# ScalarE scales the states' part of an mLSTM output, and the first unit's work is reordered

## The chip, the cores and the metric

The kernel runs on one core of a Trainium2 chip. A core has five engines that matter here, each with its own instruction queue: TensorE (PE, matmuls and transposes; PEld is its loading of weights), VectorE (DVE), ScalarE (ACT), GpSimd (POOL), and SyncE (SP), which here issues most of the DMA transfers. [...] The metric is device microseconds of one execution; several executions are made, and the median is given.

## The reference

Two blocks run one after the other. The first is an mLSTM cell over 4 batches, 8 heads, 768 tokens and a head dimension of 40; the second is a feed-forward network in which two up-projections are multiplied.

```python
for t in range(S):
    m_new = np.maximum(f_gate[:, :, t] + m, i_gate[:, :, t])
    f_stab = np.exp(f_gate[:, :, t] + m - m_new)
    i_stab = np.exp(i_gate[:, :, t] - m_new)
    m = m_new
    C = f_stab * C + i_stab * einsum('bhd,bhe->bhde', vt, kt)
    n = f_stab * n + i_stab * kt
    h_tilde = einsum('bhde,bhe->bhd', C, qt)
    denom = np.maximum(np.abs(einsum('bhd,bhd->bh', n, qt)), 1.0)
    y[:, :, t] = sigmoid(o_gate[:, :, t]) * h_tilde / denom
x = y.transpose(0, 2, 1, 3).reshape(3072, 320)
a = x @ w1                      # 320 -> 1024
b = x @ w2                      # 320 -> 1024
return ((a * b) @ w3) @ w_out   # 1024 -> 1024 -> 320
```

## The kernel before

**The cell.** Time is cut into units of 128 tokens of one batch with all 8 heads. There are 24 units; unit n is chunk n // 4 of batch n % 4. Within a unit the recurrence is written as matrix products over two halves of 64 tokens. For each head:

- The scores `ss` are k·q, multiplied by a masked weight `pw` (an exponential that ScalarE takes at L280 and GpSimd masks at L282). The product is made by VectorE at L355, straight from PSUM.
- `pc` is the unit's contribution to the state: `vw` (v times a gate weight, GpSimd, L304) times k.
- One step later, `ph` is the product of the weighted scores with v, and `pi` is the state times q. The unit's output is h = ph + pi·gT, where gT is a gate column, one value per token and head. An appended column of ones gives the denominator in the same products, so a head has 41 columns.

On VectorE the output `outputs(n)` is L377 (pi times gT, all heads in one instruction), four additions L382 (ph), three small ones on the denominator (L390 to L393), L398 (the output gate, whose tanh ScalarE takes at L263), and L400, which writes y. GpSimd then copies y's last columns (L430), and PE transposes y (`px`), which ScalarE copies to `xT` (L440).

**The feed-forward part.** The weights arrive as 64-bit words. ScalarE scales the raw words (L178), and four VectorE instructions make fp32 of them (L189 to L192). w3 and w_out are folded into one matrix w3o on the chip (`wp`, evicted by ScalarE at L257). The up-projections are the PSUM tiles `pa` and `pb`; ScalarE evicts `pa` to `a_sb` (L585) and VectorE multiplies it with `pb` into `ab` (L586).

**The steps.** A loop over s = 0 to 31 puts the two blocks beside each other. Step s issues the loads of unit s+2, transposes k and q of unit s (PE `pt`; ScalarE copies them to `kT` and `qT`, L299, for units below 10, and VectorE transposes them itself from unit 10 on), takes one fold of w3 and the up-projections (one or two pairs from step 4 on), and then calls `quarter_work(s)`. That finishes the up-projections (a_sb and ab), then issues PE's `ph` and `pi` of unit s-1, `ss` and `pc` of unit s, and the VectorE work on them. At the end of the step ScalarE takes the exps of unit s+1 and the tanh of unit s, and weights are converted and fetched.

The order of the instructions on ScalarE, VectorE, GpSimd and SyncE is the order in which the program writes them (`keep_order`), from the gate scans to step 31; PE is in order as well. PE's results other than the cell's lie in four PSUM banks, taken in rotation, so that in steps with two pairs of up-projections the first `pb` takes the bank of k's `pt` and waits until ScalarE has copied it to `kT`. The cell's own results lie in two tiles `cell` of two banks each: `ph` and `pi` in one, `ss` and `pc` in the other.

**Before the loop** VectorE scans the gates (L514 to L528), and `gate_cols` transposes the gate rows into columns `aT`, `wT` and `gT`. `spread(0)` puts the first unit's gate values into PSUM, and `weights(0)` takes the exps and masks them.

In `quarter_work` the order on VectorE before the change is: L377 and the four L382 of unit s-1, L355 of unit s, the state (L360 or L362), the denominator of unit s-1, the second state addition (L368), L398 and L400.

Of the kernel before, what the change touches and what calls it, by code (L numbers as in the profile page):

```python
# [10 lines left out]
AF = mybir.ActivationFunctionType  # L11
OP = mybir.AluOpType
# [4 lines left out]
def kernel(  # L17
# [26 lines left out]
    nc = tc.nc  # L44

    B, H, S, D = q.shape
    L = 64
# [53 lines left out]

    NB, NBQ = 4, 3
    N_DVE = 10
    q_all = const.tile([P, NBQ * H * DP], FP, name="q_all")
    qbuf = [q_all[:, i * H * DP:(i + 1) * H * DP].rearrange("p (h d) -> p h d", d=DP) for i in range(NBQ)]
    kbuf = [const.tile([P, H, DP], FP, name=f"kbuf{i}") for i in range(NB)]
# [4 lines left out]
    gT = const.tile([P, NT2, BH], FP, name="gT")  # L111
    wT = const.tile([P, NT2, BH], FP, name="wT")
# [38 lines left out]
    def weights_tile(n):  # L151
        if n not in u_t:
            u_t[n] = io.tile([P, H, L], FP, name="pw", tag="pw", bufs=5)
        return u_t[n]
# [71 lines left out]
    def scale_next():  # L226
        scaled.append(pend.pop(0))
        scale(scaled[-1][1])
# [36 lines left out]
    def spread(n):  # L265


        ub = mps([P, H, L], "ub")
        for h in range(H):
            r = n % B * H + h  # L270
            for x in range(2):
                mm(ub[halves[x], h, :], ident[0:RG, r:r + 1].to_broadcast([RG, L]), U[:, x * L:(x + 1) * L])
        return ub

    def weights(n):
        c, b = divmod(n, B)
        src = weights_tile(n) if c else spread(n)
        pw = weights_tile(n)
        for h in range(H):
            nc.scalar.activation(out=pw[:, h, :], in_=src[:, h, :], func=AF.Exp, bias=aT[:, c, b * H + h:b * H + h + 1])  # L280
        for r in halves:
            nc.gpsimd.affine_select(out=pw[r], in_=pw[r], compare_op=OP.is_ge, fill=0.0, base=0,  # L282
                                    pattern=[[0, H], [1, L]], channel_multiplier=-1)
# [17 lines left out]
    def weighted(n):  # L301
        c, b = divmod(n, B)
        vw_t[n] = sb.tile([P, H, D1], FP, name="vw", tag="vw")
        nc.gpsimd.tensor_tensor(out=vw_t[n], in0=vbuf[n % NB], op=OP.mult,  # L304
                                in1=wT[:, c, b * H:(b + 1) * H].unsqueeze(2).to_broadcast([P, H, D1]))
# [6 lines left out]
    def quarter_work(s, rest):  # L312


        rest()

        def part(j, c0, n):
            return cell[j][:, :, c0:c0 + NP * n].rearrange("p x (n d) -> p x n d", d=n)

        ss, pc, pi = part(0, 0, L), part(0, NP * L, D1), part(1, 0, D1)  # L320
        ph = [cell[1][:, x, NP * D1:2 * NP * D1].rearrange("p (h d) -> p h d", d=D1) for x in range(2)]
        n = s - 1
        if 0 <= n < NU:
            pw, vt, qT = u_t.pop(n), vbuf[n % NB], qT_t.pop(n)
            before = before_t.pop(n)

            for hd in range(H // 2):
                for x, e in quarters:
                    hq = hd if x == e else hd + H // 2
                    mm(ph[x][halves[e], hd, :], pw[halves[x], hq, :], vt[halves[x], hq, :])  # L330
            for p in range(NP):
                for hip, x in quarters:
                    mm(pi[halves[x], hip, p, :], qT[heads[hip], p, halves[x]], before[x][heads[hip], p, :])
        n, first_read = s, None
        if n < NU:
            c, b = divmod(n, B)
            kt, vw = kbuf[n % NB], vw_t.pop(n)
            ends = range(2 if c < NT2 - 1 else 1)
            first, second, after = state[b]
            before_t[n] = first, second  # L340
            state[b] = after, second, first
            kT, qT, pw = kT_t.pop(n), qT_t[n], u_t[n]
            for p in range(NP):
                for hip, x in quarters:
                    mm(ss[halves[x], hip, p, :], kT[heads[hip], p, halves[x]], qT[heads[hip], p, halves[x]])
            for p in range(NP):
                for x, e in quarters:
                    if x in ends:
                        mm(pc[halves[e], x, p, :], kt[halves[x], 2 * p + e, :], vw[halves[x], 2 * p + e, :])
        den = None  # L350
        if 0 <= s - 1 < NU:
            den = outputs(s - 1, pi, ph)
        if n < NU:
            pv = pw.rearrange("p (n two) t -> p two n t", two=2)
            first_read = nc.vector.tensor_tensor(out=pv, in0=ss, in1=pv, op=OP.mult)  # L355
        with tc.issue_after(first_read.ins) if first_read else nullcontext():
            if n < NU:

                if c:
                    nc.vector.tensor_tensor(out=second, in0=pc[:, 0], in1=second, op=OP.add)  # L360
                else:
                    nc.vector.tensor_copy(out=second, in_=pc[:, 0])  # L362
                if len(ends) > 1:
                    decayed(after, second, n, 1)
            if den:
                done = den()
            if n < NU and len(ends) > 1:
                nc.vector.tensor_tensor(out=after, in0=pc[:, 1], in1=after, op=OP.add)  # L368
            if den:
                done = done()  # L370
        return done if den else first_read

    def outputs(n, pi, ph):
        c, b = divmod(n, B)
        hs = slice(b * H, (b + 1) * H)
        h = sb.tile([P, H, D1], FP, name="h", tag="h")
        nc.vector.tensor_tensor(out=h.rearrange("p (n two) d -> p two n d", two=2), in0=pi,  # L377
                                in1=gT[:, c, hs].rearrange("p (n two) -> p two n", two=2).unsqueeze(3)
                                .to_broadcast([P, 2, NP, D1]), op=OP.mult)
        for x, e in quarters:  # L380
            part = h[halves[x], 0:H // 2] if x == e else h[halves[x], H // 2:H]
            nc.vector.tensor_tensor(out=part, in0=ph[x][halves[e]], in1=part, op=OP.add)  # L382

        den = sb.tile([P, H, 1], FP, name="den", tag="den")

        def first():
            V = nc.vector
            V.tensor_scalar(out=den.bitcast(U32), in0=h[:, :, D:D1].bitcast(U32), scalar1=0x7FFFFFFF, scalar2=None,  # L390
                            op0=OP.bitwise_and)
            V.tensor_scalar(out=den, in0=den, scalar1=1.0, scalar2=2.0, op0=OP.max, op1=OP.mult)
            V.reciprocal(out=den, in_=den)  # L393
            return then

        def then():
            e = o_t.pop(n)
            nc.vector.scalar_tensor_tensor(out=e, in0=e, scalar=1.0, in1=den.to_broadcast([P, H, D]), op0=OP.add, op1=OP.mult)  # L398
            y_t[n] = sb.tile([P, DM + REM], FP, name="y", tag="y")
            return nc.vector.tensor_tensor(out=y_t[n][:, 0:DM].rearrange("p (h d) -> p h d", d=D), in0=h[:, :, 0:D],  # L400
                                           in1=e, op=OP.mult)

        return first
# [39 lines left out]
    GR, GC = 3, NT // 3  # L443
    TC = GC * L
    RG = GR * BH
# [6 lines left out]
    w, g = f_sb, on  # L452
# [58 lines left out]
    V = nc.vector  # L511
# [19 lines left out]
    def gate_cols(src, dst, copy):  # L531
        pg = mps([P, GC // 2, GR, BH], "pg")
        for c in range(GC // 2):
            transpose(pg[:, c].rearrange("p g r -> p (g r)"), src[:, c * P:(c + 1) * P], RG)
        for c in range(GC // 2):
            copy(out=dst.rearrange("p (g c) r -> p c g r", g=GR)[:, c], in_=pg[:, c])

    turn(0)
    gate_cols(a, aT, nc.scalar.copy)
    nc.scalar.activation(out=dec, in_=U3[:, :, L - 1], func=AF.Exp)  # L540
    scale_next()
    V.tensor_tensor(out=w3d, in0=a3, in1=U3[:, :, L - 1:L].to_broadcast([RG, GC, L]), op=OP.add)
    scale_next()
    convert()
    nc.scalar.activation(out=w, in_=w, func=AF.Exp)

    for i, r in enumerate(third):
        nc.gpsimd.tensor_tensor(out=pick[r, :, i, :], in0=pair[r].to_broadcast([BH, B * NP, GC]), op=OP.mult,
                        in1=dec[r].unsqueeze(1).to_broadcast([BH, B * NP, GC]))
    weights(0)  # L550
    pd = mps([P, B * NP * NT], "pd")
    for x in range(2):
        mm(pd[halves[x]], odd[:, x].to_broadcast([RG, L]), pick.rearrange("p j g c -> p (j g c)"))
    gate_cols(w, wT, nc.scalar.copy)
    nc.scalar.copy(out=decay.rearrange("p j c -> p (j c)"), in_=pd)
    nc.scalar.activation(out=g, in_=U, func=AF.Exp)
    scale_next()
# [151 lines left out]
    for s in range(len(n_up)):  # L709
# [6 lines left out]
            weights(s + 1)  # L716
            out_gate(s)
        if s < NU:
            weighted(s)
            if s >= B:  # L720
                decayed(state[s % B][1], state[s % B][0], s, 0)
            if 0 < s < N_DVE:
                turn(s)
# [109 lines left out]
```

## Time and profile before

Three executions took 443.79, 445.97 and 446.03 us; the median is 445.97. The span of the profiled execution is 444.0 us.

| What | Value |
|---|---|
| Busy: PE, PEld | 420.7 us, 332.6 us |
| Busy: DVE, ACT, POOL | 342.8, 133.8, 81.7 us |
| Instructions: DVE, ACT, POOL | 704, 376, 154 |
| L377 (pi times gT) | 24 times, 0.490 us each |
| L382 (four additions, one unit) | 1.35 us |
| L355 (the product pw) | 0.69 us |
| L280 (exps), data in SBUF | 160 times, 0.335 us each; eight in 2.00 us |
| L280 (exps), data in PSUM | 32 times, 0.322 us each; eight in 1.71 us |
| Start of the cell's PE work in steps 7, 8, 9, 10 | 83.41, 96.73, 109.00, 126.04 us |

The profile is read in this way. Busy times are per engine and add up over the span; a share of 95% for PE says that the engine is hardly ever idle, not that it works at its peak. Neighbouring ScalarE instructions overlap, so eight exps of 0.335 us take 2.00 us and not 2.68; the distance from start to start (the pitch) is what a queue behind them feels. A view of waits lists, for an engine, what released it when it had been idle; a timeline gives each instruction's start and length, with the idle time before it in brackets.

### The profile page before, as it was taken

What the parts mean: (1) busy time and instruction counts of PE and PEld (TensorE: products, weight loads), DVE (VectorE), ACT (ScalarE), POOL (GpSimd) and SP (SyncE); (2) the same over time, 40 slices, a digit from 0 to 9 for tenths busy, and PEclk for the clock granted to TensorE, in tenths of its full rate; (3) what the DMA queues carried; (4) which work ended last, traced back from release to release, by engine and by line L of the source; (5) the groups of instructions that cost most, each with busy time, mean ns of one, the idle gap of its engine ahead of it and who ended that gap; (6) DMA issues with size and microseconds to landing.
All of it is one profiled execution on the core that took longest, in us unless ns stands there. A gap on an engine that the chain in (4) does not pass through costs nothing.

```text
span 444.0 us, 12907 instructions
## 1 busy us (share of the span) xinstructions
PE 420.7 (95%) x5271; PEld 332.6 (75%) x5271; DVE 342.8 (77%) x704; ACT 133.8 (30%) x376; POOL 81.7 (18%) x154
## 2 busy tenths in 40 slices
PE   4778998999999999999999999999999999999997
PEld 3666777788678788887877877878778777777774
DVE  6699999989998988898867859659699776444800
ACT  3655445534342244133302320213211111101110
POOL 3362433123220220222022203202010000000000
PEclk9998999999999999999999999999999999999999
DMA  8999979888988787688466477274111120000001
GB/s 204 186 184 214 191 127 165 159 193 185 194 196 191 162 169 169 157 158 154 98 113 144 94 143 144 68 132 110 50 35 35 40 45 17 15 16 15 1 30 44
DMA packets 136554, 52.71 MB, mean 119 GB/s; under 512 B 109936, under 2 KB 127536, under 8 KB 136496
## 3 DMA queue, kind: packets, MB, share of 16 engines
q1 hardware_dynamic: 132896, 47.87, 54.7%
q10 hardware_dynamic: 3600, 4.03, 2.7%
q8 instruction: 41, 0.67, 0.7%
q14 instruction: 17, 0.14, 0.1%
HBM read 46.07 MB, written 5.80 MB: 117 GB/s over the span
## 4 chain that ended last, share of the span: by engine, by line
PE 75%; DVE 8%; SPq 6%; DMA 4%; issue 2%; POOL 2%; ACT 1%; DVEq 0%; ACTq 0%; POOLq 0%
PE cell L92 22%; PE pa L92 17%; PE po L92 14%; PE pb L92 11%; PE wp L92 7%; PE p L92 5%; SPq L173 3%; DMA raw<-in_moe_w_dram 2%; DMA raw<-in_moe_w_out_dram 1%; DVE h L382 1%; DMA o_in<-in_o_gate_dram 1%; DVE pw L355 1%; DVE ex L189 1%; SPq L137 1%; DVE ma L191 1%
## 5 line engine op out<-in xcount | busy, mean ns | idle before, releaser
L92 PE MATMUL po<-w3o,ab 128*128 128x320 f32 x224 | 61.8, 433 | 0.0
L92 PE MATMUL pa<-xT,w 128*128 128x256 f32 x240 | 60.5, 383 | 0.9 <-ACT xT L440 0.8
L92 PEld LDWEIGHTS po<-w3o,ab 128*128 128x128 f32 x224 | 42.4, 190 | 17.3 <-issue 0.4
L309 POOL TENSOR_TENSOR state<-state,decay 128x164 f32<-128x164 f32 x40 | 19.7, 492 | 181.2 <-DVE den L390 178.8
L92 PEld LDWEIGHTS pa<-xT,w 128*128 128x128 f32 x240 | 44.5, 190 | 8.6 <-ACT xT L440 1.5
L92 PE MATMUL pb<-xT,w 128*128 128x256 f32 x192 | 45.6, 380 | 1.6 <-ACT kT L299 1.5
L282 POOL TENSOR_SCALAR_AFFINE_SELECT pw<-pw 64x512 f32<-64x512 f32 x48 | 35.1, 732 | 52.4 <-ACT pw L280 47.9
L92 PE MATMUL cell<-w3o,ab 128*128 128x320 f32 x160 | 44.0, 432 | 0.0
L92 PEld LDWEIGHTS pb<-xT,w 128*128 128x128 f32 x192 | 36.3, 190 | 7.2 <-ACT kT L299 2.4
L280 ACT ACTIVATE pw<-pw,aT 128x64 f32<-128x64 f32 x160 | 40.2, 336 | 2.9 <-ACT o_sb L688 2.9
L633 DVE SCALAR_TENSOR_TENSOR a_sb<-pa,wo 128x512 f32<-128x512 f32 x12 | 8.3, 691 | 42.2 <-PE pa L92 42.2
L92 PEld LDWEIGHTS cell<-w3o,ab 128*128 128x128 f32 x160 | 30.4, 190 | 12.0
L585 ACT ACTIVATE a_sb<-pa 128x512 f32<-128x512 f32 x24 | 14.3, 598 | 77.7 <-PE pb L92 77.7
L92 PE MATMUL wp<-wo,w3T 128*128 128x320 f32 x128 | 35.9, 433 | 1.0 <-DVE ab L586 1.0
L92 PE MATMUL pa<-xT,wr 64*64 64x256 f32 x384 | 36.8, 386 | 0.0
L92 PE MATMUL pb<-xT,wr 64*64 64x256 f32 x384 | 36.2, 379 | 0.0
L382 DVE TENSOR_TENSOR h<-cell,h 64x164 f32<-64x164 f32 x96 | 31.3, 326 | 1.8
L92 PEld LDWEIGHTS wp<-wo,w3T 128*128 128x128 f32 x128 | 23.7, 190 | 10.1 <-DVE ab L586 1.2
L92 PEld LDWEIGHTS pa<-xT,wr 64*64 64x64 f32 x384 | 19.0, 132 | 14.4 <-issue 8.3
L688 ACT COPY o_sb<-po 128x320 f32<-128x320 f32 x14 | 6.0, 425 | 67.4 <-PE po L92 67.4
L586 DVE TENSOR_TENSOR ab<-pb,a_sb 128x512 f32<-128x512 f32 x24 | 16.4, 688 | 8.6 <-ACT a_sb L585 8.4
L92 PE MATMUL cell<-vw,kbuf 64*64 64x41 f32 x704 | 16.4, 227 | 6.6 <-POOL vw L304 4.4
(123 smaller groups left out, 738.2 us busy)
## 6 DMA issues: line engine op xcount, KB each, us to landing
raw<-in_moe_w_dram SPq DMA_DIRECT2D x64, 128.0 KB, 3.2
pw<-U_d SPq DMA_DIRECT2D x40, 128.0 KB, 3.8
kbuf<-in_k_dram SPq DMA_DIRECT2D x24, 160.0 KB, 4.6
vbuf<-in_v_dram SPq DMA_DIRECT2D x24, 160.0 KB, 4.8
o_in<-in_o_gate_dram SPq DMA_DIRECT2D x24, 160.0 KB, 4.8
out_dram<-o_sb ACTq DMA_DIRECT2D x24, 160.0 KB, 1.8
raw<-in_moe_w_dram SPq DMA_DIRECT2D x7, 512.0 KB, 6.1
raw<-in_moe_w_out_dram SPq DMA_DIRECT2D x32, 80.0 KB, 3.3
```

The costliest lines, as they stand in the source:

```text
L92: in_order(nc.tensor.matmul(out, lhsT=lhsT, rhs=rhs, start=start, stop=stop))
L137: nc.sync.dma_start(out=dst[p0:p0 + 32, c0:c0 + NP * RAW].rearrange("r (p e) -> r p e", p=NP), in_=of.rearrange("p (r f) d -> r p (f d)", ...
L173: nc.sync.dma_start(out=dst, in_=src)
L189: V.tensor_scalar(out=t, in0=hi, scalar1=3, scalar2=None, op0=OP.logical_shift_left)
L280: nc.scalar.activation(out=pw[:, h, :], in_=src[:, h, :], func=AF.Exp, bias=aT[:, c, b * H + h:b * H + h + 1])
L282: nc.gpsimd.affine_select(out=pw[r], in_=pw[r], compare_op=OP.is_ge, fill=0.0, base=0, pattern=[[0, H], [1, L]], channel_multiplier=-1)
L309: nc.gpsimd.tensor_tensor(out=new, in0=old, op=OP.mult, in1=decay[:, b * NP:(b + 1) * NP, 2 * c + x:2 * c + x + 1] .to_broadcast([P, NP, D1]))
L382: nc.vector.tensor_tensor(out=part, in0=ph[x][halves[e]], in1=part, op=OP.add)
L585: nc.scalar.mul(out=a_sb, in_=pa, mul=UP ** -2)
L586: nc.vector.tensor_tensor(out=ab_t[gr][j][:, fs[0]:fs[-1] + 1, t0:t0 + a_sb.shape[-1]], in0=pb, in1=a_sb, op=OP.mult)
L633: nc.vector.scalar_tensor_tensor(out=out, in0=p, scalar=UP ** -2, in1=q, op0=OP.mult, op1=OP.add)
L688: nc.scalar.copy(out=o_sb, in_=po)
```

## The change

The change has two parts. For units 0 to 15 the product of the states' part with the gate column (L377) goes from VectorE to ScalarE: eight activations, one for each head, each with the head's gate column as its scale. VectorE's remaining work on the output is put off: the scores' product L355 and the state come first, then the four additions, the denominator, and the rest. In ScalarE's order the eight stand behind the step's `a_sb` evictions and ahead of the exps of the next unit, the tanh, the raw scales and the next step's copies `kT` and `qT`.

The second part is the first unit. The gate weight's exponent (`w3d`) and exp are taken ahead of the first raw scale, `spread(0)` and the transposes `wT` right behind it; GpSimd makes `vw` of unit 0 ahead of the masks of `weights(0)`, and PE makes `pd` (the decay columns) after that.

It is meant to relieve VectorE, which is busy 77% of the span, by using ScalarE, which is busy 30%, and to let the first scores' product begin earlier.

```diff
+    N_ACT = 16
...
-    def weights(n):
+    def weights(n, src=None):
         c, b = divmod(n, B)
-        src = weights_tile(n) if c else spread(n)
+        src = src or (weights_tile(n) if c else spread(n))
...
             if den:
                 done = den()
+                if s <= N_ACT:
+                    done = done()
             if n < NU and len(ends) > 1:
                 nc.vector.tensor_tensor(out=after, in0=pc[:, 1], in1=after, op=OP.add)
...
         h = sb.tile([P, H, D1], FP, name="h", tag="h")
+        if n < N_ACT:
+            for hd in range(H):
+                nc.scalar.activation(out=h[:, hd, :], in_=pi[:, hd % 2, hd // 2, :], func=AF.Copy,
+                                     scale=gT[:, c, b * H + hd:b * H + hd + 1])
+            return lambda: outputs_rest(n, h, ph)
         nc.vector.tensor_tensor(out=h.rearrange("p (n two) d -> p two n d", two=2), in0=pi,
...
+        return outputs_rest(n, h, ph)
+
+    def outputs_rest(n, h, ph):
         for x, e in quarters:
...
+    V.tensor_tensor(out=w3d, in0=a3, in1=U3[:, :, L - 1:L].to_broadcast([RG, GC, L]), op=OP.add)
+    nc.scalar.activation(out=w, in_=w, func=AF.Exp)
     scale_next()
-    V.tensor_tensor(out=w3d, in0=a3, in1=U3[:, :, L - 1:L].to_broadcast([RG, GC, L]), op=OP.add)
+    first_spread = spread(0)
+    gate_cols(w, wT, nc.scalar.copy)
     scale_next()
     convert()
-    nc.scalar.activation(out=w, in_=w, func=AF.Exp)
...
-    weights(0)
+    weighted(0)
+    weights(0, first_spread)
     pd = mps([P, B * NP * NT], "pd")
...
-    gate_cols(w, wT, nc.scalar.copy)
     nc.scalar.copy(out=decay.rearrange("p j c -> p (j c)"), in_=pd)
...
         if s < NU:
-            weighted(s)
+            if s:
+                weighted(s)
```

## The prediction

> **What bounds the kernel now.** I read the page first, then the waits of TensorE (PE) by stretches, then the timelines of ScalarE (ACT) and PE where a wait ends, then the windows. The page:
>
> ```profile
> PE 420.7 (95%) x5271; PEld 332.6 (75%) x5271; DVE 342.8 (77%) x704; ACT 133.8 (30%) x376; POOL 81.7 (18%) x154
> ```
>
> PE is busy for 420.7 of 444.0 us, so all that a change on other engines can win is some 20 us of gaps. The waits of PE between 16 and 124 us (line, releaser: us in total, times, longest):
>
> ```profile
> PE cell L92 <- POOL vw L304: 4.4, 3, 2.9
> PE cell L92 <- issue: 2.2, 3, 1.0
> PE px L95 <- POOL y L430: 1.9, 2, 1.1
> PE pb L92 <- ACT kT L299: 1.5, 1, 1.5
> PE wp L92 <- DVE ab L586: 1.0, 1, 1.0
> ```
>
> The same view from 124 to 444 us is empty: in that stretch PE waits for nothing, and nothing off PE can shorten it. So I ask one thing: does the change move the moment at which PE passes 120.6 us, after which it never waits? The windows (start:end, length; busy PE, PEld, DVE, ACT, POOL; PE clock, DMA share, GB/s):
>
> ```profile
> 30.00:40.00 10.00, 7.29 (x225) 6.33 (x218) 9.56 (x22) 5.98 (x16) 4.25 (x7) 0.83 1.06 174
> 40.00:60.00 20.00, 16.61 (x346) 13.65 (x345) 18.45 (x40) 9.26 (x26) 7.38 (x12) 1.00 1.15 192
> 100.00:124.00 24.00, 22.90 (x244) 18.20 (x243) 22.98 (x48) 9.42 (x23) 6.80 (x12) 1.00 0.95 191
> ```
>
> Up to 124 us the DMA share is about one, and DVE is busy 92 to 96% of the time. The queue of SyncE runs without a break from 9.7 to 124 us; for its transfers I looked for the last reader or writer of each buffer, and none was the reason that a transfer began (the closest was done 1.4 us earlier). So transfers, not engines, set the pace there. They pin PE at three places: A, the transposes of unit 4's k begin at 39.77, its k landing at 39.64; B, PE pb at 76.26, behind ACT, whose scaling of raw words waits for a transfer that lands at 75.14; C, the stretch before 120.61:
>
> ```profile
> 113.88 0.68 ACT L178 ACTIVATE raw<-raw 128x512 f32<-128x512 f32 x1 [1.23 <-DMA raw<-in_moe_w_dram]
> 117.78 0.69 ACT L178 ACTIVATE raw<-raw 128x512 f32<-128x512 f32 x1 [3.21 <-DMA raw<-in_moe_w_dram]
> 119.52 0.69 ACT L178 ACTIVATE raw<-raw 128x512 f32<-128x512 f32 x1 [1.05 <-DMA raw<-in_moe_w_dram]
> 120.10 0.47 ACT L440 COPY xT<-px 128x384 f32<-128x384 f32 x1
> ```
>
> Between B and C stands the place that decides, the ACT queue of step 8 and the PE groups behind it:
>
> ```profile
> 96.96 0.60 ACT L585 ACTIVATE a_sb<-pa 128x512 f32<-128x512 f32 x1 [0.27 <-PE pb L92]
> 97.45 2.00 ACT L280 ACTIVATE pw<-pw,aT 128x64 f32<-128x64 f32 x8
> 99.36 0.46 ACT L263 ACTIVATE o_in<-o_in 128x320 f32<-128x320 f32 x1
> 99.72 1.61 ACT L178 ACTIVATE raw<-raw 128x320 f32<-128x320 f32 x3
> 101.23 0.56 ACT L299 COPY kT<-pt 128x512 f32<-128x512 f32 x1
> ```
> ```profile
> 99.94 1.89 PE L92 MATMUL pa<-xT,w 128*128 128x256 f32 x8
> 101.84 1.99 PE L92 MATMUL pb<-xT,w 128*128 128x256 f32 x8
> ```
>
> ACT has no gap from the second a_sb to kT, and PE pb starts at 101.84, 0.05 after kT has freed its bank at 101.79. PE itself was ready at 101.66 (99.94 plus 8 starts of 0.2155). ACT has no slack here, though it is busy only 30% of the span.
>
> **What the Trainium skill says.** The Trainium skill, "ScalarE: Activation LUTs", section What ACT_TABLE_LOAD costs: an activation with one [128,1] pointer operand takes about 280 ns + 0.833 ns an element, and neighbours overlap by about 93. For the 64-element exps that is 333 alone and 240 from start to start; the trace has a median of 335 and a pitch of 0.239 us, so it agrees for data in SBUF. For 41 elements the page gives an estimate of 314 ns, a pitch of 0.221. "PSUM — Partial Sum Buffer", section Engine vs sequencer instructions: the queues of ScalarE, VectorE and GpSimd are strictly first in, first out, and matmuls start in program order; the timeline above agrees, kT's copy waiting behind work that has nothing to do with it. "TensorE: Matmul & The Clock Gate", Part 1: after an idle window of about 3.4 us PE runs at half rate; the clock of 0.83 in the window 30 to 40 fits.
>
> **The change, part by part.**
>
> (1) Sixteen times, 8 ACT activations of 41 elements from PSUM take the place of one DVE product. Their price is not in the trace. The first unit's exps read PSUM: 8 of 64 elements took 1.71 us, a pitch of 0.196. Raw scales of 512 and 320 elements give some 0.9 ns an element, so 23 fewer take off 0.02: pitch 0.175, eight cost **1.4 us**. Lower end 1.0 (pitch 0.13, as short copies have), upper end 1.8 to 1.9 (the page's 0.221, or 0.239 as from SBUF). I take 1.4, since source and operands match that row best. No further table load is expected: the copies of L299 already stand between exps, and the trace has one table load in all.
>
> (2) DVE loses L377, 0.49 us in each of 16 stages. The page's DVE is nearly full before 124 us, so this is time that DVE gets; but what DVE gives earlier ends at pins A, B and C.
>
> (3) Scores first: the product pw (0.69) no longer stands behind 0.49 + 1.34 us of h work, but waits for the last pc matmul, about 0.8 us after pi. y of the unit then comes about 1.35 us later relative to pw. Queued behind it are POOL's copy of y (L430) and PE's px, a step later, with a stage of 11 to 13 us between: hidden from unit 6 on.
>
> (4) First unit. The chain shows its price:
>
> ```profile
> 14.18 1.02 POOL pw L282
> 15.27 0.74 POOL vw L304
> 16.06 1.14 PE cell L92 x32
> 17.32 0.69 DVE pw L355
> ```
>
> With wT's transposes and vw ahead of the exps and selects, vw ends near 11.9 in place of 16.0, and pw's product starts near 15.4 in place of 17.32, bound by the second select: **1.9 us** earlier. Units 1 to 3 come earlier by as much, and unit 4 by nothing, since its k lands at 39.64 as before (pin A). PE idles longer before that, which costs up to one 3.4 us window at half clock.
>
> (5) What follows. After A, the waits for POOL y (0.8 and 1.1) shrink, against the ACT delay of 1.4 in each step; up to stage 6 this comes to between -0.35 and +0.5. At B the transfer decides: 0 to +0.2, as the eight stand ahead of the raw scale in the queue, long done when it lands.
> Step 7: pi ends near 84.5, the eight follow, kT moves from 88.12 to 89.9; PE pb stood at 89.68, so +0.27.
> Step 8: pi ends near 97.88, that is 0.43 after ACT was free at 97.45; 0.43 + 1.4 = 1.83 of delay, plus 0.27: kT ends near 103.9, and pb moves from 101.84 to 103.94, **+2.1**. Behind that wait PE has all of step 8's second half queued.
> Step 9: PE waited 0.97 for DVE ab (L586) before wp at 112.48. DVE is ahead by then, so this wait is eaten: +1.1. At C the transfer chain left PE 0.28 of slack (pb's eight starts from 118.61 end at 120.33; the next pa began at 120.61): **+0.85**. With B's 0 to 0.2 that gives +1.0.
> After 124 us: the eight run where ACT is about a quarter busy. The tightest, xT's eviction, has some 3.4 us of slack, so nothing is added.
> Sum: 445.97 + 1.0 = **447.0 us**.
>
> **The rivals.**
>
> R1, swallowed: the pins take both sides, as the wait of 0.97 and later slack do when the eight are cheap (1.0 us gives +0.2). Time 446.0. Against it: step 8's zero slack.
>
> R2, faster: the savings reach the end. For it: PE's waits for vw, qT, POOL y and ab sum to 8.0 us (4.4, 0.7, 1.9, 1.0), and the first unit's 1.9 us lies openly on the chain. If half of it arrives, 442.0. Against it: the transfer queue waits for no engine, so earlier engines find no earlier data; and the largest gap, 2.9 us, lies before pin A.
>
> R3, a larger loss: a pitch of 0.22 to 0.24 adds 0.4 to 0.5 in steps 7 and 8 each, so +1.6 to +2.6; with a window at half clock after A, +3.0: 449.0. ACT then becomes the bound of each step from 5 to 9. For it: the skill's pitch, and no slack in ACT's queue at two steps. Against it: B still absorbs what comes before 76 us.
>
> **How the numbers follow.** Chances: main case 0.45, R1 0.12, R2 0.16, R3 0.27. The forecast is the main case's. Range: low 443.0, inside R2's reach (three of the 8.0 us arrive; what lies below is about 0.1); high 449.5, R3 with a little more, leaving out about 0.1. The bounds of half a per cent are 443.74 and 448.20. Faster 0.16 is R2; slower is R3 with 0.05 of the main case's upper end, 0.32; the rest, 0.52, is within.
>
> **What would show it.** Right: eight activations a unit in place of L377 with a pitch of 0.17 to 0.18; PE pb in step 8 waiting for ACT kT about 2 us, a wait that is not there now; the wait for ab near 112 gone; unit 4's transposes still at 39.7; no PE waits after 124. Wrong: if PE passes its last early wait (120.61 now) earlier than before, R2 holds, and my reading of the transfers as the pace was wrong; if waits for ACT appear after 124 us, the eight cost more than their slot; if pb of step 8 does not move, ACT had slack that I didn't see.

## The result, and the profile after

The changed kernel took 452.01 us (median of 4 runs, 451.72 to 452.47), the kernel before 446.0 beside it: ratio 1.0136, 95% interval 1.0094 to 1.0177. Measured once more (run e7 below) the ratio is 1.0087, interval 1.0057 to 1.0117. So the change makes the kernel slower by about 4 to 6 us; the forecast had been +1.0 us.

The page of the changed kernel, part 1:

```profile
PE 428.9 (95%) x5271; PEld 339.9 (76%) x5271; DVE 332.2 (74%) x688; ACT 158.4 (35%) x504; POOL 81.8 (18%) x154
```

VectorE is relieved of 10.6 us (342.8 before), ScalarE takes 24.6 more (133.8). PE has the same instructions and is busy 8.2 us longer, a first sign that part of them ran at a lower clock, that is, at a smaller share of full speed than PE can be granted. The waits of PE between 16 and 124 us (line, releaser: us in total, times, longest):

```profile
PE cell L92 <- issue: 5.2, 3, 3.2
PE pb L92 <- ACT kT L300: 3.5, 2, 1.9
PE px L95 <- POOL y L441: 1.1, 1, 1.1
PE pa L92 <- ACT xT L451: 0.6, 1, 0.6
PE pt L95 <- DMA kbuf<-in_k_dram: 0.4, 1, 0.4
PE cell L92 <- POOL vw L305: 0.4, 1, 0.4
```

Lines below L101 have moved by one to thirteen. VectorE's and GpSimd's waits of before (vw 4.4, y 1.9, ab 1.0) have shrunk to 1.5; in their place stand kT on ScalarE, twice, and a wait named issue, in which PE waits for nothing that the profile shows. From 124 us on the view is empty again. The windows (start:end, length; busy PE, PEld, DVE, ACT, POOL; clock, DMA share, GB/s):

```profile
30.00:40.00 10.00, 5.90 (x168) 4.79 (x160) 7.90 (x19) 6.78 (x27) 2.86 (x5) 0.81 1.20 180
40.00:60.00 20.00, 17.85 (x224) 14.69 (x223) 12.87 (x31) 9.96 (x30) 7.04 (x12) 0.75 1.05 186
100.00:124.00 24.00, 22.10 (x390) 17.84 (x389) 20.68 (x45) 15.31 (x49) 6.55 (x11) 1.00 0.97 196
```

Between 40 and 60 us PE's clock is 0.75, where the trace of before had 1.00. VectorE is busy for 12.87 us in place of 18.45 there, but the two stretches do not hold the same work, since the changed kernel is some 3.5 us behind by then; PE gains nothing by it. The place that the forecast was about, ScalarE's queue of step 8 and what stands behind it on PE:

```profile
102.66 0.60 ACT L598 ACTIVATE a_sb<-pa 128x512 f32<-128x512 f32 x1 [0.27 <-PE pb L92]
103.58 1.60 ACT L382 ACTIVATE h<-cell,gT 128x41 f32<-128x41 f32 x8 [0.33 <-PE cell L92]
105.02 2.05 ACT L281 ACTIVATE pw<-pw,aT 128x64 f32<-128x64 f32 x8
106.93 0.49 ACT L264 ACTIVATE o_in<-o_in 128x320 f32<-128x320 f32 x1
107.29 1.61 ACT L179 ACTIVATE raw<-raw 128x320 f32<-128x320 f32 x3
108.77 0.60 ACT L300 COPY kT<-pt 128x512 f32<-128x512 f32 x1
```
```profile
105.64 1.89 PE L92 MATMUL pa<-xT,w 128*128 128x256 f32 x8
109.43 1.99 PE L92 MATMUL pb<-xT,w 128*128 128x256 f32 x8 [1.90 <-ACT kT L300]
```

The eight activations hold the queue for 1.44 us (103.58 to the first exp at 105.02), after 0.33 of waiting for pi. kT ends at 109.37, PE starts pb at 109.43 and has waited 1.90. Step 7 of this trace has no wait for kT. PE stands still there for 1.17 us before 90.36, in a wait named issue at unit 7's pc, and its clock is 0.83 between 90 and 100 us.

And the start of the program on VectorE, where the first unit's product pw stood at 17.32 before:

```profile
15.58 0.68 DVE L356 TENSOR_TENSOR pw<-cell,pw 128x512 f32<-128x512 f32 x1
```

It helps to follow one event through the steps: the start of PE's ph in step s, taken from the timelines of PE; a step's length is from its ph to the next one. "Before again" is a second trace of the kernel before (run e8), the other columns are runs of the study.

| Step | before | before again | changed | units 5 to 7 only (e12) | changed, raw scales behind kT (e15) |
|---|---|---|---|---|---|
| 4 | 48.51 | 51.55 | 52.07 | 51.43 | 53.79 |
| 6 | 69.61 | 72.65 | 73.47 | 72.61 | 74.87 |
| 7 | 83.41 | 84.65 | 87.30 | 86.42 | 87.55 |
| 8 | 96.73 | 96.95 | 102.43 | 100.23 | 100.23 |
| 9 | 109.00 | 113.01 | 116.58 | 114.39 | 112.91 |
| 10 | 126.04 | 128.44 | 132.01 | 129.81 | 130.27 |

After step 10 the distances change little: the changed kernel is 5.97 us behind the first trace of before at step 10 and 6.0 at the end. The two traces of before differ as well: step 4 starts 3 us earlier in the first. The first comes from an execution of 445.75 us, the second from one of 448.75, and the medians of the kernel before in the several measurements were 446.0 to 447.7, so the first is an early one and the second a late one. Against the second, the changed kernel is 0.5 us behind at step 4, 3.6 at step 10 and 3.0 at the end; the medians of the repeated measurement are 3.5 apart.

### The profile page after: what moved, and what is told of

Same layout as the page of the kernel before. It is cut to its first block, busy times and chain, and to the rows that moved or that the text cites. A ratio compares the mean times of both kernels' runs of the same rounds, so it can differ in the third digit from the quotient of the medians.

```text
span 450.0 us, 13031 instructions
## 1 busy us (share of the span) xinstructions
PE 428.9 (95%) x5271; PEld 339.9 (76%) x5271; DVE 332.2 (74%) x688; ACT 158.4 (35%) x504; POOL 81.8 (18%) x154
## 4 chain that ended last, share of the span: by engine, by line
PE 87%; DMA 4%; ACT 3%; SPq 2%; issue 2%; POOL 1%; DVE 0%; ACTq 0%; POOLq 0%; DVEq 0%
PE cell L92 24%; PE pa L92 20%; PE pb L92 14%; PE po L92 13%; PE wp L92 8%; PE p L92 5%; DMA kbuf<-in_k_dram 2%; PE pt L95 2%; DMA q_all<-in_q_dram 1%; PE px L95 1%; ACT pw L281 1%; SPq L174 1%; DMA pw<-U_d 1%; ACT raw L179 1%; PE ub L92 0%
## 5 line engine op out<-in xcount | busy, mean ns | idle before, releaser
L92 PE MATMUL pa<-xT,w 128*128 128x256 f32 x240 | 62.9, 394 | 0.6 <-ACT xT L451 0.6
L92 PEld LDWEIGHTS pa<-xT,w 128*128 128x128 f32 x240 | 46.2, 197 | 9.1 <-ACT xT L451 1.0
L382 ACT ACTIVATE h<-cell,gT 128x41 f32<-128x41 f32 x128 | 25.6, 313 | 6.4 <-PE cell L92 6.4
```

What stands on the lines that cost most here:

```text
L92: in_order(nc.tensor.matmul(out, lhsT=lhsT, rhs=rhs, start=start, stop=stop))
L382: nc.scalar.activation(out=h[:, hd, :], in_=pi[:, hd % 2, hd // 2, :], func=AF.Copy, scale=gT[:, c, b * H + hd:b * H + hd + 1])
```

## The experiments

Two theories stood after the first trace. **Lead**: the first unit's early start lets PE run into missing transfers and instructions at step 3, and the idle time halves its clock. **Queue**: ScalarE's eight activations hold back kT in steps 6 to 8. Ratios are to the kernel before, measured beside each run on the same chip.

**e1, the first unit's order alone; e2, the activations and scores first alone.** e1 sets N_ACT to 0; e2 puts the old order of the first unit back.

```diff
-    N_ACT = 16
+    N_ACT = 0          # e1
```
```diff
-    weighted(0)        # e2
-    weights(0, first_spread)
+    weights(0)
...
+    gate_cols(w, wT, nc.scalar.copy)
...
-            if s:
-                weighted(s)
+            weighted(s)
```

> The first unit's new order alone; L377 stays on VectorE and the output's work ahead of the scores, as before. Theory (lead): the first unit's 2 us of lead let PE run ahead of its transfers, so that at the end of step 3 it starves (for instructions at matmul pc of unit 3, and for unit 4's k), the idle time halves its clock in step 4, and step 4's ph starts 2.5 to 4 us later than the 48.51 of before. The transfer behind PE pb in step 6 takes 1.5 of that back, and the waits before 120 us some more: 446.5 to 448. Rival (ScalarE alone): the eight activations make the whole loss, and this kernel takes 445 to 446, with step 4 at 47 to 48.5.

> The eight activations and scores first for units 0 to 15, the first unit in its old order. Theory (lead): no starving at step 3, step 4's ph starts at 48 to 49; what is left is ScalarE's queue ahead of kT in steps 6 to 8, about 2 us at step 8: 447 to 448. Rival (ScalarE alone): 451 to 452, as with the whole change, and step 4 at 51 to 52.

e1: 0.9991 (0.9975 to 1.0007). e2: 1.0071 (1.0043 to 1.0100). So the first unit's order neither costs nor brings anything that can be measured; nearly the whole loss comes with the activations. The theory of the lead falls as a cause of the difference: e2 has the old first unit, and its step 4 starts at 51.26 with a wait named issue of 2.7 us all the same.

**e3, the whole change without units 5, 6 and 7.**

```diff
-                if s <= N_ACT:
+                if s <= N_ACT and s - 1 not in (5, 6, 7):
...
-        if n < N_ACT:
+        if n < N_ACT and n not in (5, 6, 7):
```

> The whole change, but units 5, 6 and 7 keep L377 on VectorE and the output's work ahead of the scores (steps 6, 7 and 8, where PE pb waits for ScalarE's kT). Theory: the loss up to step 4 stays (3.6 us), the waits for kT of 1.6 in step 6 and 1.9 in step 8 go, so 2.5 to 3.5 us less than the whole change: 448.5 to 449.5. Rival (the early lead sets the end alone): 451.5 to 452, since other waits take their place.

1.0025 (1.0008 to 1.0043), about 1.1 us. Leaving out three of sixteen units takes away most of the loss: e2, measured beside it, lost 0.71%. In its trace PE's pb waits for kT once, 0.7 us.

**e4, scores first alone**, L377 on VectorE behind the product pw, the first unit in its old order.

```diff
         if n < N_ACT:
-            for hd in range(H):
-                nc.scalar.activation(out=h[:, hd, :], ...)
-            return lambda: outputs_rest(n, h, ph)
+            def late():
+                nc.vector.tensor_tensor(out=h.rearrange(...), in0=pi, in1=gT..., op=OP.mult)
+                return outputs_rest(n, h, ph)
+            return late
```

> Scores first alone: L377 stays on VectorE but stands behind the product pw, for units 0 to 15; no activations on ScalarE, the first unit in its old order. Theory: no queue on ScalarE, no lead: 445.5 to 446.5. Rival (putting the outputs off delays y, GpSimd's copy and PE's px in the early steps): 447 or more, with PE waiting longer for POOL y before 60 us.

0.9989 (0.9973 to 1.0006): the order on VectorE is worth nothing either way.

**e7 and e8, both kernels once more.**

> The changed kernel once more, beside the others on one chip. Theory (queue, and starving at step 3 in every kernel by chance): ratio to before 1.007 to 1.010, as the eight activations alone gave (1.0071). Rival (the first unit's lead adds its own loss): 1.012 to 1.015.

> The kernel before once more, for its trace on this chip. Theory (chance): the stretch of missing instructions at unit 3's pc and the half clock in step 4 are there too in this trace, step 4's ph at 50 to 52 in place of 48.51, and the time has a spread of 3 us or more. Rival (lead): step 4's ph at 48 to 49, the clock at half for one window at most.

e7: 1.0087; e8: 0.9993 (0.9971 to 1.0014), its runs 444.65 to 450.12. The trace of e8 shows that the half clock is not the change's doing. The windows of the kernel before, second trace:

```profile
30.00:40.00 10.00, 8.03 (x208) 7.16 (x204) 9.60 (x21) 6.43 (x18) 4.59 (x7) 0.62 0.89 159
40.00:60.00 20.00, 18.08 (x224) 14.82 (x224) 16.04 (x36) 7.08 (x18) 7.38 (x12) 0.76 1.12 195
```

The clock is 0.62 and 0.76, with no change made. In the traces of the study step 4 starts at 50.9 us or later, but for one (e14, 48.17).

**e12, the activations for units 5, 6 and 7 alone**, the first unit in its old order; the edit is shown against the changed kernel.

```diff
-                if s <= N_ACT:
+                if s - 1 in (5, 6, 7):
...
-        if n < N_ACT:
+        if n in (5, 6, 7):
```

> The eight activations and scores first for units 5, 6 and 7 alone; all else as before. Theory (ScalarE's queue in steps 6 to 8): these three units carry two thirds or more of the loss: ratio 1.005 to 1.008, with PE's waits for kT of 1.5 and 1.9 us in steps 6 and 8. Rival (spread over all units): 1.001 to 1.003.

1.0037 (1.0023 to 1.0052). This is the cleanest pair with e8, since both enter step 6 at the same moment (72.61 and 72.65). ScalarE and PE in step 6 of e8, the kernel before:

```profile
73.38 2.01 ACT L280 ACTIVATE pw<-pw,aT 128x64 f32<-128x64 f32 x8
75.29 0.46 ACT L263 ACTIVATE o_in<-o_in 128x320 f32<-128x320 f32 x1
75.65 1.30 ACT L178 ACTIVATE raw<-raw 128x320 f32<-128x320 f32 x3
76.85 0.57 ACT L299 COPY kT<-pt 128x512 f32<-128x512 f32 x1
```
```profile
75.87 1.89 PE L92 MATMUL pa<-xT,w 128*128 128x256 f32 x8
77.59 1.89 PE L92 MATMUL pb<-xT,w 128*128 128x256 f32 x8
```

And of e12:

```profile
73.77 1.59 ACT L382 ACTIVATE h<-cell,gT 128x41 f32<-128x41 f32 x8 [0.33 <-PE cell L92]
75.20 2.05 ACT L281 ACTIVATE pw<-pw,aT 128x64 f32<-128x64 f32 x8
```
```profile
79.26 0.92 PE L92 MATMUL pb<-xT,w 128*128 128x256 f32 x3 [1.55 <-ACT kT L300]
```

In e8 no transfer holds the queue: kT ends at 77.42, and PE gets to pb at 77.59 by its own pace, a slack of 0.17. In e12 the exps begin 1.82 later (75.20 for 73.38), and PE waits 1.55. The step takes 13.81 us in place of 12.00. PE's waits for kT in e12 are 1.55, 0.92 and 1.90 in steps 6, 7 and 8. Its loss at the end, 0.37% or 1.7 us, is smaller than their sum of 4.4. The kernel before has losses of its own in step 8. In e8, kT stood there behind a raw scale whose transfer was late:

```profile
103.02 0.67 ACT L178 ACTIVATE raw<-raw 128x512 f32<-128x512 f32 x1 [2.03 <-DMA raw<-in_moe_w_dram]
```
```profile
104.21 3.65 PE L92 MATMUL pb<-xT,w 128*128 128x256 f32 x8 [2.15 <-ACT kT L299]
```

PE's clock was 0.83 between 100 and 110 us as well, and step 8 took 16.06 us in e8, against 14.16 in e12, where the raw scales no longer wait for a transfer. The share of these units in the whole loss, 0.37 of 0.87%, is below the two thirds that were expected; leaving them out (e3) took away 0.46 of 0.71%.

**e13, units 0 to 4 alone; e14, units 8 to 15 alone.**

```diff
-                if s <= N_ACT:
+                if s - 1 < 5:          # e13
+                if 8 < s <= N_ACT:     # e14
...
-        if n < N_ACT:
+        if n < 5:              # e13
+        if 8 <= n < N_ACT:     # e14
```

> The eight activations and scores first for units 0 to 4 alone (steps 1 to 5), the first unit in its old order. Theory (only queues ahead of kT with a full bank rotation count, steps 6 to 8): 0.999 to 1.001. Rival (early steps cost too): 1.002 to 1.004.

> The eight activations and scores first for units 8 to 15 alone (steps 9 to 16), where VectorE makes kT itself and no kT stands on ScalarE. Theory: no PE wait for kT is made, VectorE gets 0.49 us a stage back and the wait of PE wp for DVE ab goes: ratio 0.997 to 1.000. Rival (the activations cost wherever they stand): 1.001 to 1.004.

e13: 1.0011 (0.9988 to 1.0035); e14: 1.0005 (0.9992 to 1.0018). Neither is measurably slower than before, and e14 isn't faster either, although VectorE gets time back there. The three groups add up to 0.53%, against 0.71% for all sixteen units in e2; the widths of the intervals cover that gap, so whether the groups make each other worse stays open.

**e15, the whole change with raw scales behind kT; e16, the kernel before with the same order.** The transposes of units 5 to 9 are called a little earlier, behind the tanh; PE's order is the same.

```diff
-            if 0 < s < N_DVE:
+            if 0 < s <= B:
                 turn(s)
...
             out_gate(s)
+        if B <= s and s + 1 < N_DVE:
+            turn(s + 1)
```

> The whole change, with the copies kT and qT of units 5 to 9 put ahead of the raw scales only (exps and tanh stay ahead of them). Theory (ScalarE's queue ahead of kT is the loss): taking 1.2 to 1.6 us of raw scales out of kT's way gives back what the eight activations (1.43 us) put in; PE's waits for kT in steps 6 to 8 shrink to under 0.7 us each, and the ratio to before is 0.999 to 1.003. Rival (the loss lies in other places of the change): waits gone, ratio still 1.006 or more.

> The kernel before, with the same order of kT, qT and raw scales. Theory: the waits for kT that are left in before (up to 2.15 us in step 8, where a raw scale waits for its transfer) go: ratio 0.995 to 0.999. Rival (VectorE's backlog sets these stages): no difference, 0.999 to 1.001, with a longer wait of PE wp for DVE ab.

e15: 1.0012 (0.9994 to 1.0030), against 1.0087 for the same change without this edit. ScalarE in step 8 of e15:

```profile
101.39 1.60 ACT L382 ACTIVATE h<-cell,gT 128x41 f32<-128x41 f32 x8 [0.33 <-PE cell L92]
102.83 2.04 ACT L281 ACTIVATE pw<-pw,aT 128x64 f32<-128x64 f32 x8
104.74 0.49 ACT L264 ACTIVATE o_in<-o_in 128x320 f32<-128x320 f32 x1
105.10 0.60 ACT L300 COPY kT<-pt 128x512 f32<-128x512 f32 x1
```

kT starts 4.87 us after ph's start in this step (100.23); in the changed kernel it was 6.34 (108.77 from 102.43). PE's waits in e15:

```profile
PE cell L92 <- issue: 6.0, 3, 4.8
...
PE pb L92 <- ACT kT L300: 0.8, 2, 0.4
```

The waits for kT fell to 0.42 twice, and the loss with them, although the wait named issue is larger in this trace (4.8) than in any other. That is the decisive run: all activations are still there, only their place ahead of kT is made up for. e16 came out at 1.0021 (1.0004 to 1.0037), so the same order does not help the kernel before: its waits for kT go, and PE waits 2.6 us for DVE ab in step 9 instead. VectorE's backlog is the next limit in that trace, as the rival said, though 1.0021 lies just above the rival's range. Measured together, e15 and e16 give the cleanest comparison: with kT ahead of the raw scales in both, the kernel with the change took 1.0012 and the one without it 1.0021, so in that order the change costs nothing that can be measured.

The other traces agree in direction. Where the eight stood ahead of kT in steps 6 to 8, PE's waits of pb for kT sum to 3.5 us (the changed kernel), 3.9 (e2), 4.4 (e12) and 4.7 (e7). With no activations in these steps they sum to 0.7 (e3 and e13), 1.4 (e1), 1.55 (the first trace of before), 1.6 (e4), 2.15 (e8) and 2.6 (e14). On average that is an estimated 2.6 us more, a good part of the 3.2 and 3.9 us that e2 and e7 lost by their ratios; where the rest arises was not found.

**e5, e6 and e9, kT ahead of the exps too.** e5 is the changed kernel, e6 the kernel before, e9 is e6 with GpSimd's copy of y also moved ahead of the masks.

```diff
-            if 0 < s < N_DVE:
+            if 0 < s <= B:
                 turn(s)
...
-        elif 0 <= s - 2 < NY:          # e9
-            twice(s - 2)
...
+        if 0 <= s - 1 < NY:            # e9
+            twice(s - 1)
+        if B <= s and s + 1 < N_DVE:
+            turn(s + 1)
         if B - 1 <= s < NU:
             if s + 1 < NU:
                 weights(s + 1)
```

> The whole change, with the transposes of units 5 to 9 called ahead of the exps, so that ScalarE's copies kT and qT stand right behind the eight activations and ahead of exps, tanh and raw scales; PE's order is the same. Theory (queue): kT ends about 3 to 4 us earlier in steps 5 to 8, PE's waits for it (1.6, some 0.4 and 1.9 us in steps 6 to 8) go, and the kernel is level with before, 0.996 to 1.002 of it. Rival (lead): the loss comes from the early steps, the waits move elsewhere, and the ratio stays at 1.007 or more.

> The kernel before, with the same earlier copies of kT and qT for units 5 to 9. Theory (queue): the wait of PE pb for kT in step 6 (1.55 us, behind a raw scale that waits for its transfer) goes; at 120 us the transfers take some back: 0.5 to 1.5 us faster than before, ratio 0.996 to 0.999. Rival (transfers pace all): no difference, 0.999 to 1.001.

> The kernel before, with the earlier copies of kT and qT of the run before it in this study and also GpSimd's copy of y (L430) put ahead of the masks, one step earlier. Theory: PE's wait of 3.3 us for POOL y at step 5, which the earlier kT had made, goes, and so does the wait for kT: ratio 0.995 to 1.001. Rival (VectorE's own backlog of conversions sets stages 8 to 10 whatever ScalarE does): 1.002 to 1.006, with PE wp waiting for DVE ab over 1.5 us near 115.

e5: 1.0053 (1.0031 to 1.0074), e6: 1.0081 (1.0052 to 1.0111), e9: 1.0026 (1.0005 to 1.0047). e5 and e6 miss what was expected, and show how an order passes a wait on. GpSimd in step 5 of e6:

```profile
57.23 1.85 POOL L282 TENSOR_SCALAR_AFFINE_SELECT pw<-pw 64x512 f32<-64x512 f32 x2 [0.92 <-DMA pw<-U_d]
59.17 0.78 POOL L304 TENSOR_TENSOR vw<-vbuf,wT 128x328 f32<-128x328 f32 x1
59.91 0.91 POOL L309 TENSOR_TENSOR state<-state,decay 128x164 f32<-128x164 f32 x1
60.77 0.70 POOL L430 COPY y<-y 128x64 f32<-128x64 f32 x1
```

The exps now wait for PE's transposes of k and q, the masks for the exps, and y's copy stands behind the masks: PE waits 3.3 us for y in e5 and e6, where it was 1.1. (The line names a transfer as what released the masks, but the last of the exps ended at 57.16, just before they start.) With y's copy moved (e9) most of that loss goes. The traces of e9 and of e11 below come from executions that took twice the usual time, and nothing is taken from them.

**e10 and e11, one fetch of raw words a step later**, in the kernel before and in the changed one.

```diff
-(2 if s < 2 else 3 if s < ahead - 1 else 4)
+(2 if s < 1 else 1 if s < 2 else 3 if s < ahead - 1 else 4)
```

> The kernel before, with one fetch of raw words (512 KB) issued a step later, behind unit 4's k, q and v. Theory (transfers starve PE at step 3): unit 4's k and the instructions of unit 3's pc come some 3 us earlier, no gap named issue over 1 us near 38, little half clock, step 4's ph at 46 to 48.5: in the whole 0 to 2 us faster. Rival (the stretch is PE's own, not the transfers'): gap and half clock stay, step 4's ph at 51 to 52.

> The changed kernel with the same later fetch. Theory (ScalarE's queue): PE's waits for kT in steps 6 to 8 stay at 1.5, some 0.4 to 1.2 and 1.9 us, and it is 2 to 4 us slower than the kernel before with that fetch. Rival (the loss needs the starving at step 3): it is level with that kernel, within 0.2%.

e10: 1.0043 (1.0026 to 1.0061); e11: 1.0079 (1.0055 to 1.0102). In e10 the wait named issue near 39 us is down to 0.18 us. That says little for the theory of the transfers, since e8, without the later fetch, has only 0.26 there. The half clock stays (0.50 between 35 and 50 us), and the late raw words hold up ScalarE's queue in step 3 so that PE waits 4.3 us for xT at 43.4. Step 4 starts at 55.08, worse than before. The difference of e11 and e10, 0.36%, is between what the two theories gave, and decides nothing.

## Why the prediction was wrong

**What held.** The price of the activations (part 1): eight were put at 1.4 us in the queue, at a pitch of 0.175; the trace shows a pitch of 0.178 and 1.43 to 1.44. The estimate of 0.221 worked out from the Trainium skill, "ScalarE: Activation LUTs", section What ACT_TABLE_LOAD costs, was too high for these operands in PSUM; the 314 ns estimated from it for a single one agrees with the 0.310 of the trace. Step 8 (part 5): PE pb was to wait about 2 us for kT, and waits 1.90. The first unit (part 4): pw's product was to start near 15.4, it starts at 15.58, and the gain is swallowed, as e1 shows. The wait for ab is gone in the changed kernel's trace, and nothing waits after 124 us.

**The step that failed** is in part 5: "At B the transfer decides: 0 to +0.2". In the trace I worked from, step 6 started at 69.61, and kT waited there for a raw scale and its transfer, 1.55 us of room in which eight activations would cost nothing:

```profile
76.26 1.99 PE L92 MATMUL pb<-xT,w 128*128 128x256 f32 x8 [1.55 <-ACT kT L299]
```

But the second trace of before enters step 6 at 72.65, with the transfer in place, and the room is 0.17. There the eight make PE wait 1.55 in e12, and 1.56 or 1.57 in every other trace that has them ahead of the raw scales in step 6 (the changed kernel twice, and e2). Step 7, put at +0.27, had a wait of 0.42 in e2, 0.92 in e12 and 1.23 in e7, and none in the changed kernel's first trace, where PE was late through the wait named issue shown above. So the sum over steps 6 to 8 is 1.55 + 0.92 + 1.90 = 4.4 us (e12) and not the 2.1 forecast for steps 7 and 8 together plus B's 0 to 0.2.

**Why the room was not there.** It depended on when step 6 began. With no activations in step 6, PE waits there for kT 1.55 us when the step begins at 69.61 (before), 1.58 at 71.09 (e14), 0.37 at 72.20 (e1) and not at all at 72.65 (e8): begun later, the step finds the transfer done. And it often begins later, because PE runs at half clock for ten microseconds and more ahead of step 4's ph, without the change (e8) as well as with it. The kernel before then catches up: from step 4 at 51.55 to step 8 at 96.95, only 0.2 behind its first trace. It does so because PE's steps 6 and 7 run at PE's own 12.0 and 12.3 us. The changed kernel can't, since ScalarE's queue makes those steps 13.8 us (e2, e7, e12 and the changed kernel's first trace, but for its step 7 of 15.1). At step 8 it is 5.5 us behind e8; 3.6 are left at step 9, after e8's own loss in step 8. I took the pins of one trace for floors of the kernel; they were the slack that the kernel lives on.

**Two readings that failed beside it.** Unit 4's transposes (pin A) were to begin at 39.7 still. They begin at 41.38 in the changed kernel and at 40.68 in e8, without a wait for k. And "transfers, not engines, set the pace" up to 124 us was read from windows with a DMA share of 0.95 to 1.15, while between 60 and 110 us the same trace shows 0.76 to 0.92.

**Rival R3** (a larger loss) was right in direction and named the right engine, "ACT then becomes the bound of each step from 5 to 9", but gave a wrong reason, a higher pitch, and put it at +3.0, against the 4 to 6 measured. The line against it, "B still absorbs what comes before 76 us", was the failed step again. The range ended at 449.5, too low, because it was built from errors in the price and one window at half clock, and none in the starting moments of the steps.

**Scores first** (part 3) and the relief of VectorE (part 2) were rightly put at nothing that reaches the end: e4 and e14 are level with before.

## What to carry to other kernels

An engine that is busy 30% can still have no room at the one moment that matters. Look at its queue between two fixed events of the bounding engine: what is ahead of the eviction that frees PE's next bank, to the tenth of a microsecond. When work is moved onto such a queue ahead of that eviction, something else there may have to go behind it: putting raw scales behind kT turned a loss of 0.87% into 0.12%, within its error of none. More of the same was no better: with kT ahead of the exps too, the wait passed on to y, and the loss was 0.53% (e5). Putting the eight activations themselves behind kT was not run.

Before counting a wait as room that will absorb a delay, look whether a second execution of the same kernel shows it. Here the wait for a transfer in step 6 was gone once the steps before it were late.

## What the runs showed of the hardware

**PE can starve for instructions.** The wait named issue at unit 3's pc, in the changed kernel's trace:

```profile
37.10 0.27 PE L92 MATMUL cell<-vw,kbuf 64*64 64x41 f32 x8
40.57 0.88 PE L92 MATMUL cell<-vw,kbuf 64*64 64x41 f32 x24 [3.20 <-issue]
```

Counted in all of PE's instructions in the trace (weight loads, matmuls and semaphore instructions), it stops behind number 1217, and in the first trace of before a shorter gap sits behind the same number. Two other gaps named issue sit behind 961 and 2753 in both traces; all are multiples of 256 apart. The page shows what moves in these steps:

```profile
q8 instruction: 41, 0.67, 0.7%
```

That is 41 packets of 16 KB, and PE's 10,618 instructions make 41 blocks of 256 and a rest. In the changed kernel's trace one of the packets starts at 37.41, when PE has already stopped, and has landed at 39.00; PE goes on at 40.57. In all 16 traces from executions of the usual time, PE pauses behind number 1217 and goes on 1.3 to 1.8 us after such a packet has landed. The Trainium skill, "Runtime: NRT & Kernel Launch", section Instruction fetch mechanics, says that instructions are refilled in 16 KiB blocks of 256 and that this is mostly hidden. The blocks fit the trace; hidden it is not here, with stops of up to 4.8 us (e15). Whether the data transfers delay the blocks is not shown: the DMA share was 1.0 to 1.2 between 30 and 40 us in these two traces, but the stops of 1.0 and 1.2 us behind number 2753 stand where it was 0.76 and 0.77 (80 to 90 us), and e10, which moved one fetch, has a wait of 0.18 us behind number 1217 against 0.26 in e8, which moved none.

**Half clock is common ahead of step 4's ph.** The windows show 0.75 and 0.76 between 40 and 60 us with and without the change. I had expected it at most as a cost of the change, after a stretch in which PE stands idle. In the changed kernel a half clock does follow the stop of 3.2 us (0.50 between 40 and 45). In e8 it is there before the stop behind number 1217: 0.75 between 30 and 35 us and 0.50 from 35 to 45, while the longest idle time of PE between 26 and 35 us was 1.1 us. What brings it about stays open.
